# First chunk of the attention stage: shorter warming, decay factors broadcast in pieces, one large constant copied on the chip, loads and first products in another order

## Chip, cores and metric

The kernel runs on one core of one Trainium2 chip. The metric is device microseconds of one execution; the figure for a kernel is the median of its timed runs.

## What is computed

Attention with a decaying state over 768 tokens (2 batches, 8 heads of 64), then two layers of experts with routing. Only the first part is touched by the change.

```python
gamma = 1.0 - 2.0 ** (-5.0 - np.arange(H))            # one decay per head
for t in range(S):
    state = gamma * state + outer(k[:, :, t], v[:, :, t])
    y[:, :, t] = scale * einsum('bhd,bhde->bhe', q[:, :, t], state)
x = _moe_ref(x=y, ...)       # top-1 expert of 8, skip where x @ w_skip <= 0
out = _moe2_ref(x=x, ...)    # top-1 expert of 8 with a capacity per expert
```

## The kernel before

The attention works in 6 chunks of 128 tokens. For a chunk `c` and a batch `b`, `scores` (L622) multiplies keys and queries of the 8 heads: 8 products of 64 rows by 128 columns, in fp32, which the trace shows as 16 records, into two PSUM tiles `s` (4 heads each). VectorE multiplies each of the two with a decay mask (`p`, L631). `outs` (L672, from the second chunk on also L663) multiplies `p` with the values, ScalarE copies the result to `xt` (L679). `state` (L646) adds keys times values to the PSUM tile `u`, and ScalarE copies that to `sbd` (L653) for the next chunk. A generator (`sink`, of the routing) takes a finished chunk and puts its products between those of the next: `logits` (L389, copied by ScalarE to `lgs`, L393), sums (L399), transposes (L407).

The order on every engine is the order of the program text (`manual_schedule`); each engine takes its instructions in order and waits where a semaphore says so. Loads are issued by SP's queue (`nc.sync`) and by ScalarE's (`nc.scalar`); eight semaphores for loads are handed out in turn, and a load that gets one again waits in its queue for the load that had it before. A PSUM tile `s` takes one of four banks. Which one is fixed when the program is built.

What stands at the start of the program:

- ScalarE's queue issues two rows of 512 decay factors (`grow`, L107) and the columns with the triangle, the decays by position `GV` and by chunk `GS` of the constants `cs` (L108, 200 columns). SP's queue issues queries and keys of chunk 0 (L100, one load for each batch), values and keys with tokens first (L102).
- VectorE clears `zb`; TensorE then makes 7 products of `zb` with itself (`warm`, L548, 512 columns in bf16), whose results are not used.
- TensorE multiplies a column of ones with each of the two rows (`grow`), so that the decay factors stand on all 128 partitions (L571, two products of 512 columns with one row, fp32). VectorE makes the 8 masks from them (L573). A product of `zb` clears `u` (L577).
- `scores(0, 0)`; then `main(0, 0)`: `constants` (L143 to L147: the 512 columns `GQ` of query decays, 256 KB; the other 584 columns of constants; `wgt`; `cap_i`; one row of `table`), then queries and keys of chunk 1 (L77), then the further loads; `scale_k` (L598) and `decays` (L608) on GpSimd; `scores(0, 1)`, `outs(0, 0)`.
- `main(0, 1)`: `outs(0, 1)`, `state(0)`, `scores(1, 0)`.

Of the kernel before, what the change touches and what calls it, by code (L numbers as in the profile page):

```python
# [7 lines left out]
F32 = mybir.dt.float32  # L8
# [3 lines left out]
ACTF = mybir.ActivationFunctionType  # L12
# [29 lines left out]
def kernel(  # L42
# [12 lines left out]
    nc = tc.nc  # L55
# [18 lines left out]
    def load_qk(c, a_p):  # L74

        t = qk_tile(a_p)
        nc.sync.dma_start(out=t, in_=qkv[c, :, 0:2])  # L77
        return t
# [24 lines left out]
        return qk, kv  # L103

    grow = a_p.tile([128, 512], F32, name="grow", bufs=1)
    for i in (0, 64):
        nc.scalar.dma_start(out=grow[i:i + 1, :], in_=cst[i:i + 1, C_GQ:C_GQ + 512])  # L107
    nc.scalar.dma_start(out=cs[:, C_MASK:C_ID], in_=cst[:, C_MASK:C_ID])  # L108
    first = load_first()
    wgt = const.tile([128, KT, 32], F32, name="wgt")  # L110
    cap_i = const.tile([1, 2], I32, name="cap_i")
    zb = const.tile([128, 2 * RW], BF16, name="zb")
    nc.vector.memset(zb, 0.0)
    ones = const.tile([128, 128], BF16, name="ones")
    nc.vector.memset(ones, 1.0)
    a0 = const.tile([128, RW], F32, name="a0")

# [22 lines left out]
    ids_0 = const.tile([128, 2], I32, name="ids_0")  # L140

    def constants():
        nc.sync.dma_start(out=cs[:, C_GQ:C_MASK], in_=cst[:, C_GQ:C_MASK])  # L143
        nc.sync.dma_start(out=cs[:, C_ID:C_N], in_=cst[:, C_ID:C_N])
        nc.sync.dma_start(out=wgt, in_=wg)
        nc.sync.dma_start(out=cap_i, in_=capacity.bitcast(I32))
        nc.sync.dma_start(out=table[0:1, :], in_=zb[0:1, :].bitcast(F32))  # L147
# [397 lines left out]
    def warm(acc, n):  # L545

        for _ in range(n):
            nc.tensor.matmul(out=acc, lhsT=zb[:, 0:128], rhs=zb[:, 0:512], start=True, stop=True)  # L548


    def attention(a_p, ps, first, sink, pump, take_kv, give_kv, grow):
        units = [(c, b) for c in range(NCH) for b in range(B)]
        qk, kv, pt, xt = {}, {}, {}, {}
        sbd = [a_p.tile([128, B, 4, 128], F32, tag=f"sbd{i}", name="sbd", bufs=1) for i in range(2)]
# [3 lines left out]
        def psum(tag="m", bufs=2):  # L558
            return ps.tile([128, 512], F32, tag=tag, bufs=bufs, name=tag)
# [1 line left out]

        u = ps.tile([128, B, 4, D], F32, tag="u", bufs=1, name="u")
        if pump:
            warm(psum("s", 4), 7)

        mask = a_p.tile([128, 2, 4, 128], F32, name="mask", bufs=1)
        row1 = a_p.tile([128, 128], F32, name="row1", bufs=1)
        nc.gpsimd.memset(row1, 1.0)
        for j in range(2):
            g = psum("s", 4)  # L570
            nc.tensor.matmul(out=g, lhsT=row1[64 * j:64 * j + 1, :], rhs=grow[64 * j:64 * j + 1, :], start=True, stop=True)  # L571
            for r in range(4):
                nc.vector.scalar_tensor_tensor(  # L573
                    out=mask[:, j, r, :], in0=g[:, 128 * r:128 * r + 128], scalar=cs[:, C_GV + 2 * r + j:C_GV + 2 * r + j + 1],
                    in1=cs[:, C_MASK:C_MASK + 128], op0=ALU.mult, op1=ALU.mult,
                )
        nc.tensor.matmul(  # L577
            out=u.rearrange("p b r e -> p (b r e)"), lhsT=zb[:, 0:128], rhs=zb[:, 0:512], start=True, stop=True, skip_group_check=True
        )
        side, sunk = [], set()  # L580

        def step_side(c, b):
# [103 lines left out]
        def main(c, b):  # L686
            if b == 0:
                if c == 0:
                    if pump:
                        constants()  # L690
                        derived()
                    qk[1] = load_qk(1, a_p)
                    scale_k(0)
                    decays(1)
                if c + 1 < NCH:
                    kv[c + 1] = load_kv(c + 1, take_kv())
                if c + 2 < NCH:
                    qk[c + 2] = load_qk(c + 2, a_p)
                if pump and c:
                    kept[0] = c < NCH - 1  # L700
                    load_w()
                yield from scores(c, 1)
                if c and c + 1 < NCH:
                    decays(c + 1)
                if c == 0 and pump:
                    derived_late()
                if c:
                    yield from state(c)
                yield from outs(c, 0)
                return  # L710
            if c == 0:
                yield from outs(c, 1)
                yield from state(c)
            if c + 1 < NCH:
                yield from scores(c + 1, 0)
            if c:
                yield from outs(c, 1)
            give_kv(kv.pop(c))

        for _ in scores(0, 0):  # L720
# [5 lines left out]
            for _ in g:  # L726
                pass

    attention(a_p, psa, first, route_tokens(rowc, a_p), pump, take_kv, give_kv, grow)
    at.close()  # L730
    later[0] = 0

# [397 lines left out]
    def general(gctx):  # L1130
# [15 lines left out]
        with (  # L1146
            tc.tile_pool(name="ga", bufs=2) as ga_p,
            tc.tile_pool(name="gps", bufs=2, space=bass.MemoryType.PSUM) as gps,
        ):
            def take():  # L1150
                return ga_p.tile([128, 2, B, 512], F32, tag="kv", name="kv")

            grow = cs[:, C_GQ:C_GQ + 512]
            attention(ga_p, gps, (load_qk(0, ga_p), load_kv(0, take())), sink, None, take, lambda t: None, grow)
        ps = gctx.enter_context(tc.tile_pool(name="ps2", bufs=2, space=bass.MemoryType.PSUM))

        def psum(tag="t", bufs=2):
# [166 lines left out]
```

## Time and profile before

| | us |
|---|---|
| median of 3 timed runs | 398.36 |
| lowest and highest | 397.52, 399.19 |
| the profiled execution | 395.72 |
| its span, first to last instruction | 393.9 |

The profiled execution takes 1.8 us more than its span; the sums that follow are made against it. Times in the rows are microseconds from the start of the span. The lines that are read from its page and its trace stand in a section of their own below. In them PE is TensorE's products and PEld its loading of weights, DVE is VectorE, ACT ScalarE, POOL GpSimd, and SPq and ACTq are the queues of SP and ScalarE that issue loads.

### The profile page before, as it was taken

The page shows a single profiled execution, that of the slowest core. Times are in us where ns is not written, and L with a number is a line of the kernel's source. Part 1 is how long each engine was busy: PE and PEld are TensorE (multiplying, and loading weights), DVE is VectorE, ACT ScalarE, POOL GpSimd, SP SyncE. Part 2 cuts the span into 40 slices and gives each one's busy share as a digit, 9 for nine tenths or more (in the row PEclk, how much of TensorE's full clock was granted, in tenths as well). Part 3 has the DMA queues.
Part 4 walks back from the last instruction along what each step waited for, and adds up shares of the span by engine and source line. Part 5 has one row for each costly group of instructions (what it writes and reads, how often), then busy time and mean ns, then how long its engine had stood idle before and what let it go on. Part 6 is the DMA issues. An engine that isn't in the chain of part 4 may idle for free. (4 is left out here: it accounts for less than half of the span.)

```text
span 393.9 us, 6866 instructions
## 1 busy us (share of the span) xinstructions
PE 376.5 (96%) x2664; PEld 309.0 (78%) x2664; DVE 244.8 (62%) x437; ACT 210.5 (53%) x319; POOL 119.9 (30%) x184
## 2 busy tenths in 40 slices
PE   8999999899989999998999999999999999999992
PEld 4788887786667677676567998989989898898981
DVE  3657767498889869869535964654826476373200
ACT  1435655388778748747326753636636465462201
POOL 3678854262504402202143201304022040311102
PEclk9999999999999999999999999999999999999997
DMA  8999973899999998889844773965739377110101
GB/s 303 416 419 404 333 251 146 278 329 376 347 426 351 303 352 307 286 314 311 292 162 117 264 276 113 277 245 175 252 136 342 126 229 275 61 54 5 48 3 41
DMA packets 18175, 95.98 MB, mean 244 GB/s; under 512 B 2449, under 2 KB 2705, under 8 KB 8664
## 3 DMA queue, kind: packets, MB, share of 16 engines
q1 hardware_dynamic: 12196, 80.85, 56.5%
q0 software_dynamic: 3280, 9.76, 8.0%
q10 hardware_dynamic: 2660, 4.86, 3.3%
q8 instruction: 23, 0.38, 0.4%
q14 instruction: 16, 0.13, 0.1%
HBM read 87.03 MB, written 9.48 MB: 245 GB/s over the span
## 5 line engine op out<-in xcount | busy, mean ns | idle before, releaser
L251 DVE TENSOR_TENSOR lo<-big,hi 128x1024 fp32r<-128x1024 f32 (+1 forms) x126 | 147.5, 1185 | 60.9 <-ACT hi L248 60.0
L248 ACT ACTIVATE hi<-big 128x1024 fp32r<-128x1024 f32 (+1 forms) x126 | 124.6, 1013 | 3.8 <-DMA big<-in_w2a_dram 1.7
L784 PE MATMUL s<-xh,lo 128*128 128x256 f32 x224 | 63.4, 283 | 0.0
L783 PE MATMUL s<-xl,hi 128*128 128x256 f32 x224 | 63.4, 283 | 0.0
L782 PE MATMUL s<-xh,hi 128*128 128x256 f32 x224 | 63.4, 283 | 0.0
L905 POOL DMA_INDIRECT out_dram<-y,ixo x16 | 18.6, 1162 | 142.4 <-ACT y L900 139.4
L782 PE MATMUL o<-hi,hTh 128*128 128x512 f32 x112 | 44.9, 401 | 0.0
L783 PE MATMUL o<-lo,hTh 128*128 128x512 f32 x112 | 44.4, 396 | 0.0
L784 PE MATMUL o<-hi,hTl 128*128 128x512 f32 x112 | 44.4, 396 | 0.0
L782 PEld LDWEIGHTS s<-xh,hi 128*128 128x128 f32 x224 | 42.9, 191 | 0.3
L783 PEld LDWEIGHTS s<-xl,hi 128*128 128x128 f32 x224 | 42.9, 191 | 0.3
L784 PEld LDWEIGHTS s<-xh,lo 128*128 128x128 f32 x224 | 42.9, 192 | 0.0
L1084 ACT ACTIVATE hTh<-s 128x512 fp32r<-128x512 f32 x28 | 16.8, 598 | 41.0 <-PE s L784 41.0
L1085 DVE SCALAR_TENSOR_TENSOR hTl<-s,hTh 128x512 fp32r<-128x512 f32 x28 | 19.3, 691 | 30.5 <-ACT hTh L1084 30.3
L790 PE MATMUL s<-hi,xh 128*128 128x512 f32 x80 | 34.3, 429 | 1.6 <-DVE xl L377 0.9
L900 ACT ACTIVATE y<-o,rowc 128x512 f32<-128x512 f32 (+1 forms) x15 | 10.1, 674 | 47.6 <-issue 30.6
L790 PE MATMUL s<-lo,xh 128*128 128x512 f32 x80 | 31.5, 394 | 0.0
L879 POOL TENSOR_SCALAR rhsb<-m,cs 128x8 bf16<-128x8 bf16 x8 | 2.5, 306 | 81.1 <-DVE se L320 76.6
L790 PE MATMUL o<-hi,hTh 128*128 128x512 f32 x64 | 26.6, 415 | 0.0
L790 PE MATMUL o<-lo,hTh 128*128 128x512 f32 x64 | 25.3, 396 | 0.0
L784 PEld LDWEIGHTS o<-hi,hTl 128*128 128x128 f32 x112 | 21.1, 188 | 5.1
L790 PE MATMUL s<-hi,xl 128*128 128x512 f32 x80 | 25.1, 394 | 0.0
(162 smaller groups left out, 635.6 us busy)
## 6 DMA issues: line engine op xcount, KB each, us to landing
big<-in_w1a_dram SPq DMA_DIRECT2D x16, 1024.0 KB, 7.7
big<-in_w2a_dram SPq DMA_DIRECT2D x16, 1024.0 KB, 7.2
big<-in_w1b_dram SPq DMA_DIRECT2D x16, 1024.0 KB, 7.1
big<-in_w2b_dram SPq DMA_DIRECT2D x16, 1024.0 KB, 5.1
qk<-in_qkv_dram SPq DMA_DIRECT2D x5, 1024.0 KB, 10.2
big<-in_qkv_dram SPq DMA_DIRECT2D x5, 1024.0 KB, 12.0
table<-rowc ACTq DMA_DIRECT2D x5, 516.0 KB, 6.3
table<-row ACTq DMA_DIRECT2D x8, 258.0 KB, 7.2
```

The lines of the kernel that those rows point to most:

```text
L248: nc.scalar.activation(out=hi[:, k], in_=r3[:, k], func=ACTF.Copy)
L251: nc.vector.tensor_tensor(out=lo[:, k], in0=r3[:, k], in1=hi[:, k].bitcast(F32), op=ALU.subtract)
L782: nc.tensor.matmul(out=acc, lhsT=a[0], rhs=w[0], start=first, stop=False)
L783: nc.tensor.matmul(out=acc, lhsT=a[0], rhs=w[1], start=False, stop=False)
L784: nc.tensor.matmul(out=acc, lhsT=a[1], rhs=w[0], start=False, stop=last)
L790: nc.tensor.matmul(out=acc, lhsT=a, rhs=w, start=first and i == 0, stop=last and i == len(todo) - 1)
L879: nc.gpsimd.tensor_scalar(out=rhs[:, 0, :], in0=m, scalar1=p1, scalar2=None, op0=ALU.mult)
L900: nc.scalar.activation(out=y[:, 0:n], in_=acc[:, 0:n], func=ACTF.Copy, scale=xs[:, GCOL + 1:GCOL + 2])
L905: new = nc.gpsimd.indirect_dma_start(out=out[:, :], out_offset=bass.IndirectOffsetOnAxis(ap=ix, axis=0), in_=y, in_offset=None, bounds_che ...
L1084: nc.scalar.activation(out=hi[:, g:g + 2, :], in_=acc, func=ACTF.Relu)
L1085: nc.vector.scalar_tensor_tensor(out=lo[:, g:g + 2, :], in0=acc, scalar=0.0, in1=hi[:, g:g + 2, :].bitcast(F32), op0=ALU.max, op1=ALU.subtract
```

## The change

Five edits, all in the first chunk.

- `warm` makes 3 products, and the product that clears `u` follows directly.
- The rows `grow` come by one load of two rows, issued behind the constants that the masks need; that load holds 136 columns (triangle and the 8 columns of `GV` of chunk 0). The two broadcasts are made as four products of 256 columns, the first halves of both tiles first. The masks are made in turn for the one tile and the other. The column of ones (`row1`) is set by VectorE.
- The 512 columns `GQ` are no longer loaded: ScalarE copies them from the two broadcast tiles (two copies of 64 partitions by 512). The other constants come in one load of 648 columns, `GS` and the further `GV` with them.
- Queries and keys of chunk 1 are issued ahead of the constants, in two loads.
- In the first chunk `state(0)` stands behind `scores(1, 0)`.

```diff
+    nc.scalar.dma_start(out=cs[:, C_MASK:C_GV + 8], in_=cst[:, C_MASK:C_GV + 8])
+    nc.scalar.dma_start(out=grow[0:128:64, :], in_=cst[0:128:64, C_GQ:C_GQ + 512])
-    for i in (0, 64):
-        nc.scalar.dma_start(out=grow[i:i + 1, :], in_=cst[i:i + 1, C_GQ:C_GQ + 512])
-    nc.scalar.dma_start(out=cs[:, C_MASK:C_ID], in_=cst[:, C_MASK:C_ID])
...
     def constants():
-        nc.sync.dma_start(out=cs[:, C_GQ:C_MASK], in_=cst[:, C_GQ:C_MASK])
-        nc.sync.dma_start(out=cs[:, C_ID:C_N], in_=cst[:, C_ID:C_N])
+        nc.sync.dma_start(out=cs[:, C_GV + 8:C_N], in_=cst[:, C_GV + 8:C_N])
...
-            warm(psum("s", 4), 7)
-        ...
-        for j in range(2):
-            g = psum("s", 4)
-            nc.tensor.matmul(out=g, lhsT=row1[64 * j:64 * j + 1, :], rhs=grow[64 * j:64 * j + 1, :], start=True, stop=True)
-            for r in range(4):
-                nc.vector.scalar_tensor_tensor(...)      # mask[:, j, r] from g[:, 128 r:...]
+            warm(psum("s", 4), 3)
         nc.tensor.matmul(
             out=u.rearrange("p b r e -> p (b r e)"), lhsT=zb[:, 0:128], rhs=zb[:, 0:512], start=True, stop=True, skip_group_check=True
         )
+        g = [psum("s", 4) for j in range(2)]
+        for r in (0, 2):
+            for j in range(2):
+                nc.tensor.matmul(
+                    out=g[j][:, 128 * r:128 * r + 256], lhsT=row1[64 * j:64 * j + 1, :],
+                    rhs=grow[64 * j:64 * j + 1, 128 * r:128 * r + 256], start=True, stop=True,
+                )
+        for r in range(4):
+            for j in range(2):
+                nc.vector.scalar_tensor_tensor(...)      # mask[:, j, r] from g[j]
+        if pump:
+            for j in range(2):
+                pp = slice(64 * j, 64 * j + 64)
+                nc.scalar.activation(out=cs[pp, C_GQ:C_GQ + 512], in_=g[j][pp, :], func=ACTF.Copy)
...
                 if c == 0:
+                    qk[1] = qk_tile(a_p)
+                    for i in range(B):
+                        nc.sync.dma_start(out=qk[1][:, :, i], in_=qkv[1, :, 0:2, i])
                     if pump:
                         constants()
                         derived()
-                    qk[1] = load_qk(1, a_p)
...
             if c == 0:
                 yield from outs(c, 1)
-                yield from state(c)
             if c + 1 < NCH:
                 yield from scores(c + 1, 0)
             if c:
                 yield from outs(c, 1)
+            else:
+                yield from state(c)
```

On TensorE, from the broadcasts to the first products with values, with what each instruction waits for (DMAHW is a load, DVE is VectorE). L622 are the first and the second score of chunk 0, L672 the products with values. Before:

```order
L571 MATMUL s<-grow,row_137 128x512 [waits DMAHW0_49,Pool_49]
L571 MATMUL s<-grow,row_137 128x512 [waits DMAHW2_49]
L577 LDWEIGHTS zb
L577 MATMUL u<-zb 128x512
L622 MATMUL s<-qk 128x128 [waits DMAHW1_49]
L622 MATMUL s<-qk 128x128 [waits PE_49]
L622 MATMUL s<-qk 128x128 x6
L622 MATMUL s<-qk 128x128 [waits DMAHW3_49,DVE_49,PE_49]
L622 MATMUL s<-qk 128x128 [waits DVE_49,PE_49]
L622 MATMUL s<-qk 128x128 x6
L672 MATMUL m<-p,big_85 64x128 [waits DMAHW5_49,DVE_49]
L672 MATMUL m<-p,big_85 64x128 [waits DVE_49]
```

After, with L629 for the scores and L679 for the products with values:

```order
L565 MATMUL u<-zb 128x512
L573 MATMUL s<-grow,row_103 128x256 [waits DMAHW2_49,DVE_49]
L573 MATMUL s<-grow,row_103 128x256 x3
L629 MATMUL s<-qk 128x128 [waits DMAHW1_49]
L629 MATMUL s<-qk 128x128 [waits PE_49]
L629 MATMUL s<-qk 128x128 x6
L629 MATMUL s<-qk 128x128 [waits DMAHW3_49,DVE_49]
L629 MATMUL s<-qk 128x128 [waits DVE_49]
L629 MATMUL s<-qk 128x128 x6
L679 MATMUL m<-p,big_85 64x128 [waits DMAHW4_49]
L679 MATMUL m<-p,big_85 64x128 x7
```

The second score waits for VectorE in both, for another instruction of it: before, the program gives it the banks of the two broadcasts, and its wait is for the masks; after, it gives it the two banks of the first score, and its wait is for the two masked products of batch 0. The products with values of batch 0 waited for these masked products before and have no such wait left.

On ScalarE, at the start. Before:

```order
L107 DMA grow<-in_cst_dram 1x512 x2
L108 DMA cs<-in_cst_dram 128x200
L163 ACT_TABLE_LOAD
L163 ACTIVATE lc<-cs 128x256 [waits DMAHW0_49]
L679 ACTIVATE xt<-m 128x512 [waits PE_49] x2
```

After:

```order
L106 DMA cs<-in_cst_dram 128x136
L107 DMA grow<-in_cst_dram 2x512
L586 ACT_TABLE_LOAD [waits DVE_49]
L586 ACTIVATE cs<-s 64x512 [waits PE_49]
L586 ACTIVATE cs<-s 64x512 [waits DVE_49,PE_49]
L163 ACTIVATE lc<-cs 128x256 [waits DMAHW0_49]
L686 ACTIVATE xt<-m 128x512 [waits PE_49] x2
```

The two copies stand ahead of `lc`, and the load of ScalarE's table now stands behind a wait for VectorE's masks.

On SP's queue, the loads of chunk 1 and the constants. Before:

```order
L102 DMA big_85<-in_qkv_dram 128x1024 x2
L143 DMA cs<-in_cst_dram 128x512
L144 DMA cs<-in_cst_dram 128x584
L145 DMA wgt<-in_wg_dram 128x128
L146 DMA cap_i<-in_capacity_dram 1x2
L147 DMA table<-zb 1x516
L77 DMA qk<-in_qkv_dram 128x2048
```

After:

```order
L102 DMA big_85<-in_qkv_dram 128x1024 x2
L698 DMA qk<-in_qkv_dram 128x2x512 x2
L144 DMA cs<-in_cst_dram 128x648
L145 DMA wgt<-in_wg_dram 128x128
L146 DMA cap_i<-in_capacity_dram 1x2
L147 DMA table<-zb 1x516
L82 DMA big_86<-in_qkv_dram 128x2048
```

The 1 MB of chunk 1 stands ahead of the constants, and the load of 256 KB is gone.

## Rows read from the trace of the kernel before

**Rows 1.** Page: span; busy time, share of the span and instructions of each engine.

```profile
span 393.9 us, 6866 instructions
...
PE 376.5 (96%) x2664; PEld 309.0 (78%) x2664; DVE 244.8 (62%) x437; ACT 210.5 (53%) x319; POOL 119.9 (30%) x184
```

**Rows 2.** Stretches: length, busy time (instructions) of PE, PEld, DVE, ACT, POOL, PEclk, DMA, GB/s.

```profile
6.50:9.80 3.30, 3.30 (x27) 2.81 (x27) 2.75 (x9) 0.00 (x0) 0.89 (x1) 1.00 1.06 401
...
16.00:60.00 44.00, 43.65 (x599) 36.66 (x600) 31.14 (x86) 23.10 (x52) 33.82 (x42) 1.00 0.93 357
60.00:394.00 334.00, 318.55 (x1936) 263.36 (x1934) 207.53 (x334) 182.60 (x259) 79.58 (x120) 0.99 0.64 224
```

**Rows 3.** Waits of the whole run: who waited for whom, total, times, longest.

```profile
PEld t L860 <- DVE row L846: 6.2, 7, 1.5
...
PE t L860 <- DVE row L846: 4.0, 6, 1.1
```

**Rows 4.** TensorE in order of time: start, length, line, shape, count.

```profile
1.45 3.17 PE L548 MATMUL s<-zb 128*128 128x512 bf16 x7 [1.45 <-DVE zb L113]
4.55 2.08 PE L571 MATMUL s<-grow,row 1*128 1x512 f32 x4
6.56 0.61 PE L577 MATMUL u<-zb 128*128 128x512 bf16 x1
7.10 3.52 PE L622 MATMUL s<-qk 64*128 64x128 f32 x32
...
16.15 0.59 PE L399 MATMUL s<-zsum,lgs 128*128 128x18 f32 x4 [0.34 <-ACT lgs L393]
...
22.84 1.16 PE L622 MATMUL s<-qk 64*128 64x128 f32 x16
```

**Rows 5.** TensorE, order of time, window 7.09 to 8.9: the first score alone.

```profile
7.10 2.08 PE L622 MATMUL s<-qk 64*128 64x128 f32 x16
```

**Rows 6.** Score line L622, shortest, median, longest ns: window 7 to 9.7, then 13 to 20.

```profile
L622 PE MATMUL s<-qk x23: 417/418/579, 7.1 to 9.6; 64*128 64x128 f32 x23
```
```profile
L622 PE MATMUL s<-qk x32: 272/272/373, 13.9 to 18.3; 64*128 64x128 f32 x32
```

**Rows 7.** TensorE's weight loads in order of time: products with values, batches 0 and 1.

```profile
10.54 1.06 PEld L672 LDWEIGHTS m<-p,big 128*64 128x64 f32 x18
11.93 0.74 PEld L672 LDWEIGHTS m<-p,big 128*64 128x64 f32 x13 [0.32 <-DVE p L631]
```

**Rows 8.** VectorE in order of time: masks, masked products of chunk 0 and of chunk 1.

```profile
6.66 2.16 DVE L573 SCALAR_TENSOR_TENSOR mask<-s,cs 128x128 f32<-128x128 f32 x8 [5.12 <-PE s L571]
9.21 2.67 DVE L631 TENSOR_TENSOR p<-s,mask 128x512 f32<-128x512 f32 x4 [0.39 <-PE s L622]
...
15.84 1.29 DVE L631 TENSOR_TENSOR p<-s,mask 128x512 f32<-128x512 f32 x2 [3.40 <-PE s L622]
```

**Rows 9.** ScalarE in order of time, its queue's loads among it.

```profile
0.73 0.79 ACTq L107 DMA_DIRECT2D grow<-in_cst_dram  x2
...
1.94 1.28 ACT L163 ACT_TABLE_LOAD   x1 [1.94 <-issue]
10.24 0.42 ACT L163 ACTIVATE lc<-cs 128x256 bf16<-128x256 f32 x1 [7.02 <-DMA cs<-in_cst_dram]
11.68 0.60 ACT L679 ACTIVATE xt<-m 128x512 f32<-128x512 f32 x1 [1.03 <-PE m L672]
```

**Rows 10.** GpSimd in order of time: key scaling, decays of chunk 1.

```profile
8.91 2.04 POOL L598 TENSOR_TENSOR big<-big,cs 128x512 f32<-128x512 f32 x2 [5.82 <-DMA big<-in_qkv_dram]
10.91 1.04 POOL L608 TENSOR_TENSOR gqc<-cs 128x512 f32<-128x512 f32 x1
```

**Rows 11.** Loads by line: count, KB each, median us from issue to landing.

```profile
qk<-in_qkv_dram SPq DMA_DIRECT2D x2, 512.0 KB, 3.8
```

**Rows 12.** SP's queue in order of time: start and length of its first two issues.

```profile
0.73 0.95 SPq L100 DMA_DIRECT2D qk<-in_qkv_dram  x2
```

More of the change, by code (lines that the diff above doesn't have):

```diff
@@ L114 @@
     ones = const.tile([128, 128], BF16, name="ones")
+    row1 = a_p.tile([128, 128], F32, name="row1", bufs=1)
+    nc.vector.memset(row1, 1.0)
     nc.vector.memset(ones, 1.0)
@@ L548, in warm, with attention @@
             nc.tensor.matmul(out=acc, lhsT=zb[:, 0:128], rhs=zb[:, 0:512], start=True, stop=True)
-    def attention(a_p, ps, first, sink, pump, take_kv, give_kv, grow):
+    def attention(a_p, ps, first, sink, pump, take_kv, give_kv, grow, row1):
         units = [(c, b) for c in range(NCH) for b in range(B)]
@@ L563, in attention @@
         if pump:
-            warm(psum("s", 4), 7)
-        mask = a_p.tile([128, 2, 4, 128], F32, name="mask", bufs=1)
-        row1 = a_p.tile([128, 128], F32, name="row1", bufs=1)
-        nc.gpsimd.memset(row1, 1.0)
-        for j in range(2):
-            g = psum("s", 4)
-            nc.tensor.matmul(out=g, lhsT=row1[64 * j:64 * j + 1, :], rhs=grow[64 * j:64 * j + 1, :], start=True, stop=True)
-            for r in range(4):
[L573 to L576, printed above, removed]
+            warm(psum("s", 4), 3)
         nc.tensor.matmul(
@@ L579, in attention @@
         )
+        mask = a_p.tile([128, 2, 4, 128], F32, name="mask", bufs=1)
+        g = [psum("s", 4) for j in range(2)]
[7 more added lines that the diff above has]
+            for j in range(2):
+                nc.vector.scalar_tensor_tensor(
+                    out=mask[:, j, r, :], in0=g[j][:, 128 * r:128 * r + 128], scalar=cs[:, C_GV + 2 * r + j:C_GV + 2 * r + j + 1],
+                    in1=cs[:, C_MASK:C_MASK + 128], op0=ALU.mult, op1=ALU.mult,
+                )
+        if pump:
+            for j in range(2):
+                pp = slice(64 * j, 64 * j + 64)
+                nc.scalar.activation(out=cs[pp, C_GQ:C_GQ + 512], in_=g[j][pp, :], func=ACTF.Copy)
         side, sunk = [], set()
@@ L727, in attention @@
                 pass
-    attention(a_p, psa, first, route_tokens(rowc, a_p), pump, take_kv, give_kv, grow)
+    attention(a_p, psa, first, route_tokens(rowc, a_p), pump, take_kv, give_kv, grow, row1)
     at.close()
@@ L1151, in take @@
                 return ga_p.tile([128, 2, B, 512], F32, tag="kv", name="kv")
+            row1 = ga_p.tile([128, 128], F32, name="row1", bufs=1)
+            nc.vector.memset(row1, 1.0)
             grow = cs[:, C_GQ:C_GQ + 512]
-            attention(ga_p, gps, (load_qk(0, ga_p), load_kv(0, take())), sink, None, take, lambda t: None, grow)
+            attention(ga_p, gps, (load_qk(0, ga_p), load_kv(0, take())), sink, None, take, lambda t: None, grow, row1)
         ps = gctx.enter_context(tc.tile_pool(name="ps2", bufs=2, space=bass.MemoryType.PSUM))
```

## Prediction

> **What bounds the kernel now.** First the busy shares: TensorE is busy for 376.5 of 393.9 us, VectorE for 62% [rows 1]. Then the stretches: from 16 us on TensorE is busy in 43.65 of 44 us and in 318.55 of 334 us [rows 2]. Its largest waits are for routing rows that VectorE makes, 6.2 and 4.0 us in all on its two rows [rows 3], and these come out of TensorE's own earlier products. So nothing behind the first chunk takes up a delay: what the first 16 us gain or lose, the end gains or loses. Last I read the first 16 us in order of time. There the chain is: broadcasts from 4.55, masks from 6.66 to 8.82, masked products of the first score from 9.21, TensorE's products with values of batch 0 at 10.54 and of batch 1 at 11.93, the latter behind a wait for VectorE [rows 4, 7, 8]. The two scores run at half speed: a record takes 417 ns against 272 later, and a whole score 2.08 us against 1.16 [rows 4 to 6]. The seven warming products take about 0.43 us each (3.17 us for seven, the last one's end counted in) [rows 4], which is 512 columns at 1.2 GHz; the later scores run at 2.4. The column of granted clock says 1.00 there all the same [rows 2], so here I read the level from the lengths.
>
> **The change part by part.** Times are those of the profiled execution (395.72 us, span 393.9); I take the difference over to the median of 398.36.
>
> *Warming and the broadcasts.* Four warming products fewer are 1.7 us of TensorE work, but the broadcasts start at 4.55 and there is no row that shows whether they waited for the seventh product or for the second row of factors. That row was the second load of ScalarE's queue and is again the second load there [rows 9], so I keep 4.55 and let TensorE stand from about 3.2 on. Bounds: at best the broadcasts start at 3.2, 1.35 us earlier; at worst the factors land with the second half of the first queries, which is issued at about 1.2 [rows 12] and takes 3.8 us or more [rows 11]: landing at 5.0 to 5.9, 0.5 to 1.4 us later. Four products of 256 columns are as many columns as two of 512: no change. Halving them starts no mask earlier, since the first mask waits for its whole tile; the program counts the wait to the third of the four products. The masks therefore end at 8.82 as before (6.66 + 2.16). Clearing `u` earlier lets the first score start at 6.56 in place of 7.10 and end at 6.56 + 2.08 = 8.64, ahead of the masks. So the masked products of batch 0 start at 8.82, not 9.21, and two of them take 1.29 us [rows 8]: they end at 10.11. So far 0.39 us gained.
>
> *The new wait.* The second score now writes the banks of the first, and so waits for these masked products: its first products may start about 9.5, the rest at 10.11. Before, it followed the first score without a pause (32 records in 3.52 us) [rows 4]. Queued behind it on TensorE are the products with values, and VectorE's masked products of batch 1 wait for it. At the lower clock the score ends at 10.11 + 2.08 = 12.19, at the higher at 10.11 + 1.16 = 11.27. Add 1.29 for the masked products: 13.48 or 12.56, and 0.05 for the hand-over, as between 10.50 and 10.54 before. The products of batch 1 then start at 13.53 or 12.61 against 11.93: 1.60 or 0.68 us lost. The products of batch 0 fill the gap between: 1.06 us at the higher clock [rows 7], up to twice that at the lower, where they end some 0.3 us behind the masked products.
>
> *Which clock.* The trace shows one rise, at about 9.8 us within the second score, after products without a pause since 6.56, with 417 ns up to 9.6 [rows 4, 6]. In the changed kernel TensorE stands at about 3.2 to 4.5 and again from 8.4 to 10.1, so I take the rise to come behind the second score. The Trainium skill, TensorE: Matmul & The Clock Gate, Part 1, says that the low clock is the default, that sustained activity releases it, and that the point is not tied to the kernel's start; this trace agrees as far as one rise at 9.8 can. By that rule the pause costs the low clock for the second score (400.0 below), by the row alone, the same moment, it would not (398.7).
>
> *First states behind the next score.* TensorE stood 0.34 us before L399 for the `lgs` copy, which ScalarE made behind four `sbd` copies [rows 4]. With the states behind the logits, the copy is made while the states run: 0.34 us gained. The score of chunk 1 no longer comes in two halves around the logits; no other cost.
>
> *Queries ahead of the constants, 256 KB less.* The constants land at about 10.2 now (`lc` waited for them) [rows 9]. One MB ahead of them costs about 2.6 us at 401 GB/s [rows 2], the dropped 256 KB give back 0.6: about 12.2. `lc` then ends at 12.6 and the two `xt` copies queue behind it; the first now starts at 11.68 [rows 9], the logits need the second, which can't start before 14.4 here. Hidden; if the new wait did not exist, `lc` would be just in time. GpSimd waits for the same load with the decays of chunk 1: from 12.2, 1.04 us, then three short sums, done by about 14.2; the query scaling has the score of chunk 1 to wait for, about 15.6; the scaling of keys, 8.91 to 10.95, stays as it is [rows 10]. The earlier queries are used only because that score is moved forward. Less traffic gives nothing: TensorE waits for no load in the 16 to 60 us where the queues are full [rows 2].
>
> *The copies of decays.* ScalarE's table load, 1.28 us and out of the way at 1.94 before [rows 9], stands behind the last but one mask (8.6); two copies of at most 0.6 each follow: done near 11.1. Their readers are the decays (12.2) and the score of chunk 1 (14.4), which takes those two banks. Nothing; uncovered it would be up to 1.3 us.
>
> Sum: 1.60 - 0.34 = 1.26 us later, 0.3 more for the products of batch 0 at the low clock: 1.6. In the profiled execution 397.3, on the median 400.0. Its own bounds: 1.2 if the rise comes just behind the second score, 2.5 if the low clock also covers the products of batch 1 and part of the next score (a score there costs 0.92 more): 399.6 to 400.9.
>
> **The rivals.**
> - *The clock rises at the same moment.* Then 0.68 - 0.34 = 0.34 us lost: 398.7. For it: the first score still runs before 9.8; the trace can't say what the rise needs. Against: two pauses that were not there.
> - *The factors land early.* The broadcasts follow the fourth product at 3.2 and everything moves 1.35 us forward: 1.6 - 1.35, or with the early rise 0.34 - 1.35, gives 398.6 to 397.4, say 398.0. For it: the two loads are small; against: the first queries, 512 KB, are issued with them and take 3.8 us.
> - *Slower: the factors land late.* Issued behind a load of 128 pieces, they land with the second half of the first queries, at 5 to 6 us. From a landing past 4.9 on, each tenth goes straight into masks, masked products and second score; an estimate in the middle is 1.6 + 1.0, 401.0, up to 401.7. For it: the load engines are full from 6.5 us on (1.06) [rows 2]. Against: the place in ScalarE's queue is the same.
> - *The change does less than it says*, in that the masks start no earlier, is part of the forecast.
>
> **How the numbers follow.** Forecast 0.45 (400.0), same moment of the rise 0.22 (398.7), factors early 0.08 (398.0), factors late 0.25 (401.0). A measurement of this kernel tells about 0.5% from no change, 2.0 us: 396.4 to 400.35. Slower than that: nearly all of the late case, 0.24, and the upper third of the forecast's bounds, 0.14: 0.38. Faster: an early landing with an early rise and more than I see, 0.03. The rest, 0.59, is the same. The range goes from 398.2, half of the early case and a little of the same-moment case left out, to 401.7, the end of the late case.
>
> **What would show it.** In the trace after: the masks end at about 8.8 (they start with the third broadcast's end); the second score starts only behind the second masked product, with TensorE standing more than 1 us ahead of it; the length of its records (417 or 272 ns) tells the clock; no wait of L399 for `lgs`; `lc` at about 12.2 with nobody waiting for it; the table load behind the masks. It would be wrong if the second score follows the first without a pause, if the broadcasts start before 4 or behind 5, or if the distance at 16 us is not that at the end.

## The result, and the profile after

The changed kernel takes 399.98 us (median), the kernel before 397.49 beside it on the same chip: ratio 1.0059, with an interval of 1.0035 to 1.0082, so 1.4 to 3.3 us and most likely 2.3 us slower (the two medians lie 2.5 apart). The forecast was 1.6 us slower. The profiled execution took 397.37 us (span 395.6), 1.65 us more than the one of before (395.72), but it is the lowest of the kernel's 19 times, so its span is no second confirmation of the 1.6.

The page of after, its span and busy shares (compare [rows 1]), then the longest waits (compare [rows 3]). Line numbers have moved: L860, L846 are now L870, L856; L622, L672, L631 are L629, L679, L638; L571 is L573, L573 is L579.

```profile
span 395.6 us, 6872 instructions
PE 375.8 (95%) x2664; PEld 310.0 (78%) x2664; DVE 243.6 (62%) x438; ACT 211.9 (54%) x321; POOL 120.4 (30%) x183
```
```profile
PE t L870 <- DVE row L856: 3.2, 6, 1.0
PE s L573 <- DMA grow<-in_cst_dram: 2.8, 1, 2.8
...
PE s L629 <- DVE p L638: 0.8, 1, 0.8
```

Two of the three waits are new: for the factors, 2.8 us, and for VectorE's masked products, 0.8 us. The place is seen in TensorE's first 20 us in order of time (start, length, line, shape, count, idle time before it and who ended it), against [rows 4, 5, 7]:

```profile
6.17 2.08 PE L573 MATMUL s<-grow,row 1*128 1x256 f32 x8 [2.83 <-DMA grow<-in_cst_dram]
8.18 2.08 PE L629 MATMUL s<-qk 64*128 64x128 f32 x16
11.06 2.67 PE L629 MATMUL s<-qk 64*128 64x128 f32 x16 [0.80 <-DVE p L638]
13.66 2.44 PE L679 MATMUL m<-p,big 128*64 128x128 f32 x32
16.03 1.16 PE L629 MATMUL s<-qk 64*128 64x128 f32 x16
...
18.77 0.62 PE L399 MATMUL s<-zsum,lgs 128*128 128x18 f32 x4
...
19.97 0.66 PE L407 MATMUL s<-cs,xt 128*128 128x128 f32 x4
```

The broadcasts start at 6.17 and not at 4.55, behind the factors' load. The second score no longer follows the first but starts 0.80 us behind it. The router's logit sums (L399) wait no more for `lgs`. The router's transposes (L407) start at 19.97, against 17.31 before: 2.66 us later. These transposes are the mark by which the runs below are compared. VectorE and ScalarE beside it ([rows 8, 9]):

```profile
8.25 2.16 DVE L579 SCALAR_TENSOR_TENSOR mask<-s,cs 128x128 f32<-128x128 f32 x8 [6.58 <-PE s L573]
10.32 1.28 DVE L638 TENSOR_TENSOR p<-s,mask 128x512 f32<-128x512 f32 x2
13.36 1.29 DVE L638 TENSOR_TENSOR p<-s,mask 128x512 f32<-128x512 f32 x2 [1.76 <-PE s L629]
```
```profile
1.22 1.09 ACTq L107 DMA_DIRECT2D grow<-in_cst_dram  x1
10.23 1.28 ACT L586 ACT_TABLE_LOAD   x1 [10.23 <-DVE mask L579]
11.53 1.21 ACT L586 ACTIVATE cs<-s 64x512 f32<-64x512 f32 x2
12.76 0.42 ACT L163 ACTIVATE lc<-cs 128x256 bf16<-128x256 f32 x1
```

The four masked products stood in one row of 2.67 us before; now 1.76 us lie between the pairs, in which VectorE waits for the second score. ScalarE's two copies and its table load stand behind the masks. TensorE waits for none of them; GpSimd's decays of chunk 1 do, 1.62 us, but no product waits for these.

### The profile page after: what moved, and what is told of

Same layout as the page of the kernel before. It is cut to its first block, busy times and chain, and to the rows that moved or that the text cites. A ratio compares the mean times of both kernels' runs of the same rounds, so it can differ in the third digit from the quotient of the medians.

```text
span 395.6 us, 6872 instructions
## 1 busy us (share of the span) xinstructions
PE 375.8 (95%) x2664; PEld 310.0 (78%) x2664; DVE 243.6 (62%) x438; ACT 211.9 (54%) x321; POOL 120.4 (30%) x183
```

## The experiments

A profile is one execution; a time with its interval is from many. "Transposes" is the start of the router's transposes in the profile, 17.31 in the kernel before and 19.97 in the changed one.

### The bank wait: taken out, and put in alone

In the changed kernel the broadcasts take banks of the other tag:

```diff
-        g = [psum("s", 4) for j in range(2)]
+        g = [psum() for j in range(2)]
```

> The changed kernel with its two broadcast tiles in the two banks of the outputs, so that the second score gets banks of its own. Theory (the second score waits for the masked products only because of the banks): it follows the first without a pause, near 10.2 us in place of 11.06 to 11.65, the products with values of batch 1 start near 13.7 in place of 14.8, and the time falls by about 1 us (ratio to the kernel before 1.003 to 1.004). Rival (the wait is hidden behind the late masks): the products with values of batch 1 start within 0.3 us of before and the time stays at 1.006.

TensorE in order of time in this run:

```profile
7.96 3.79 PE L629 MATMUL s<-qk 64*128 64x128 f32 x32
11.95 2.58 PE L679 MATMUL m<-p,big 128*64 128x128 f32 x32 [0.21 <-ACT cs L586]
...
18.39 0.66 PE L407 MATMUL s<-cs,xt 128*128 128x128 f32 x4
```

The two scores are one row of 32 products again, though the factors are as late as in the changed kernel (the first score at 7.96, there at 8.18). The transposes come 1.58 us earlier, and the time is 397.26 us, ratio 0.9996 (0.9969 to 1.0023). The time falls by more than expected (1.003 to 1.004): at the transposes 1.08 us of the loss are left, which the time does not show. The other half of the test is the kernel before with this wait and nothing else:

```diff
-            sa = [psum("s", 4), psum("s", 4)]
+            sa = held.pop() if (c, b) == (0, 1) else [psum("s", 4), psum("s", 4)]
+            if not c and not b:
+                held.append(sa)
```

> The kernel before with the new wait alone: the second score of the first chunk is written into the two banks of the first one, everything else as it was. Theory (the forecast's step on the wait): the first score from 7.10, masks to 8.82, masked products of batch 0 9.21 to 10.5; the second score begins 9.85 with one bank and goes on at 10.5 with the other, at the low clock to 12.6, masked products of batch 1 to 13.9, products with values of batch 1 at 13.95 against 11.93: 2.0 us later there and at the transposes (19.3), and 1.5 to 2.0 us in the whole time, ratio 1.004 to 1.005. Rival A (the wait costs no clock, the rise stays near 10 us): second score 10.5 to 11.7, products of batch 1 at 13.05, 1.1 us later, ratio 1.003. Rival B (a delay in the first 16 us is taken up later): transposes 2 us late, time the same within 0.2%.

```profile
9.95 2.67 PE L624 MATMUL s<-qk 64*128 64x128 f32 x16 [0.78 <-DVE p L633]
12.55 3.48 PE L674 MATMUL m<-p,big 128*64 128x128 f32 x32
...
20.34 0.66 PE L407 MATMUL s<-cs,xt 128*128 128x128 f32 x4
```

The score starts and lasts as forecast. The products with values take 3.48 us (2.44 in the changed kernel, 3.68 in a run below, just behind a stretch with a granted clock of 0.50), so they lie mostly at the low level too, and the transposes are 3.03 us late and not 2.0. Since the rise of the clock moves from execution to execution (last section), this one profile does not show how much of the further 1.0 us is the wait's. The time is 1.0034 (1.0003 to 1.0065), 0.1 to 2.6 us: slower, as forecast, but the interval holds rival A's 1.003 too; it is the 2.67 us of the second score, at the low level, that speak against that rival. Both halves say that the wait is real. By the middle of the intervals, taking it out gives back all that the change lost (1.0059 to 0.9996), and put in alone it costs a little over half of it.

### The late factors: place, form, and both costs out

The two single rows ahead of the constants again, as before the change:

```diff
+    for i in (0, 64):
+        nc.scalar.dma_start(out=grow[i:i + 1, :], in_=cst[i:i + 1, C_GQ:C_GQ + 512])
     nc.scalar.dma_start(out=cs[:, C_MASK:C_GV + 8], in_=cst[:, C_MASK:C_GV + 8])
-    nc.scalar.dma_start(out=grow[0:128:64, :], in_=cst[0:128:64, C_GQ:C_GQ + 512])
```

> The changed kernel with its two rows of decay factors loaded as before: two loads, first in ScalarE's queue, the constants behind them. Theory (the factors came late because they stand behind the constants' load): the broadcasts start near 4.55 us in place of 6.17, the masks end near 8.8 in place of 10.41, the second score starts at 10.1 in place of 11.06 to 11.65, and the time falls by 1.0 to 1.6 us against the changed kernel (ratio to the kernel before 1.002 to 1.004). Rival (the place in the queue is not the cause): the broadcasts stay at 6 us and the time at 1.006.

```profile
6.60 2.08 PE L630 MATMUL s<-qk 64*128 64x128 f32 x16
9.45 2.67 PE L630 MATMUL s<-qk 64*128 64x128 f32 x16 [0.78 <-DVE p L639]
12.05 3.29 PE L680 MATMUL m<-p,big 128*64 128x128 f32 x32
...
19.21 0.66 PE L408 MATMUL s<-cs,xt 128*128 128x128 f32 x4
```
```profile
1.54 0.36 ACTq L108 DMA_DIRECT2D cs<-in_cst_dram  x1
```
```profile
6.44 2.17 DVE L580 SCALAR_TENSOR_TENSOR mask<-s,cs 128x128 f32<-128x128 f32 x8 [4.77 <-DMA cs<-in_cst_dram]
```

(The last two rows are of ScalarE's queue and of VectorE.) Broadcasts, masks and first score move forward by 1.6 us and more, the masks now behind their constants; the bank wait stays (0.78 us). The transposes come at 19.21, only 0.76 us earlier than in the changed kernel: the products with values now lie mostly ahead of the clock's rise and take 3.29 us in place of 2.44. Ratio 1.0048 (1.0015 to 1.0081), which can't be told from the changed kernel's, nor from the expected 1.002 to 1.004: here the trace decides and not the time. Next, the one load of both rows kept, but put first:

```diff
+    nc.scalar.dma_start(out=grow[0:128:64, :], in_=cst[0:128:64, C_GQ:C_GQ + 512])
     nc.scalar.dma_start(out=cs[:, C_MASK:C_GV + 8], in_=cst[:, C_MASK:C_GV + 8])
-    nc.scalar.dma_start(out=grow[0:128:64, :], in_=cst[0:128:64, C_GQ:C_GQ + 512])
```

> The changed kernel with its one load of both rows of factors put ahead of the load of masks and decays on ScalarE's queue: place and form of that load told apart. Theory (place: it came late because it stood behind 128 pieces): it lands by 4.5, as the two single rows did (4.44 before, 4.56 with the rows first), all four broadcasts lie between 3.2 and 6.4, masks 6.3 to 8.5 behind the other load, the bank wait as with the rows first (second score 9.3 to 9.5). Rival (form: one load that takes both rows from 64 partitions apart is slow by itself): it lands at 5.5 or later, as in the changed kernel (6.03, 5.81 and 5.86 in its three profiles), the masks start at 7.6 or later and the second score at 10.4 or later.

TensorE, ScalarE's queue and VectorE in this run:

```profile
4.47 2.08 PE L573 MATMUL s<-grow,row 1*128 1x256 f32 x8 [1.14 <-DMA grow<-in_cst_dram]
```
```profile
0.73 1.11 ACTq L106 DMA_DIRECT2D grow<-in_cst_dram  x1
1.89 0.36 ACTq L107 DMA_DIRECT2D cs<-in_cst_dram  x1
```
```profile
8.20 2.16 DVE L579 SCALAR_TENSOR_TENSOR mask<-s,cs 128x128 f32<-128x128 f32 x8 [6.53 <-DMA cs<-in_cst_dram]
```

The factors are there at 4.47: the place made them late, as the theory has it. The trace's records of the single packets on ScalarE's queue show the same: in the changed kernel the 128 pieces of the constants start from 2.56 to 4.20 and the two rows of factors only at 5.30 and 5.41; here both rows start at 3.8. The form seems to cost too: the issue of this load takes 1.11 us, against 0.79 for both single loads [rows 9], and the load behind it is then issued at 1.89 (1.54 with the single rows). The masks wait for that load until 8.20, against 6.44 with the rows first. By the packets, 0.5 of these 1.76 us are a later start (5.18, and 4.68 with the rows first); for the rest its 128 pieces take longer, to 7.57 in place of 5.90, and why is open in this one execution. Nothing is won: the transposes come 0.97 us later than in the changed kernel; the one execution took 399.14 us. Last, rows first and own banks together (the two diffs above):

> The changed kernel with both suspected costs taken out at once: the factors come as two loads of one row each ahead of the constants, and the broadcasts take the two banks of the other tag, so that the second score needs not wait for the masked products of the first. Theory (the loss is the late factors plus the bank wait, and the two add up): with the rows at 4.5 and the constants at 6.3, as with the rows alone, masks 6.4 to 8.6, first score 6.6, second score directly behind it at 8.6 to 8.7, and from there the distances of the run with own banks (9.24 us from the first score to the router's logit sums): logit sums at 15.8, transposes at 17.0, 0.3 us ahead of before (17.31) and 1.4 ahead of the run with own banks alone (18.39). Time 0.3 us under before, ratio 0.997 to 1.000. Rival A (the start of the first chunk gives nothing to the end, as the run with own banks, whose transposes were 1.1 us late and whose time was that of before, suggests): the time is that of the run with own banks, 1.000, though the transposes come 1.4 us earlier. Rival B (the queries of chunk 1 or the constants, which land at 11.7 to 13, come too late for the earlier work): TensorE stands before the score of chunk 1 and the transposes stay at 17.6 or later.

```profile
6.36 3.79 PE L630 MATMUL s<-qk 64*128 64x128 f32 x32
10.15 2.46 PE L680 MATMUL m<-p,big 128*64 128x128 f32 x32
...
16.71 0.66 PE L408 MATMUL s<-cs,xt 128*128 128x128 f32 x4
```

Time 395.81 us, ratio 0.9963 (0.9939 to 0.9986): faster than the kernel before. This version beats both. With the two costs out, the rest of the change is worth 0.60 us at the transposes in this profile and 0.6 to 2.4 us in the time. Rival A has little left: over own banks alone the transposes gained 1.68 us and the ratio 0.0033, or 1.3 us, though the two intervals still overlap.

### The warming products and the clock

Three warming products in the kernel before, in place of seven; ten in the changed kernel, in place of three; six with rows first and own banks:

```diff
-            warm(psum("s", 4), 7)
+            warm(psum("s", 4), 3)
...
-            warm(psum("s", 4), 3)
+            warm(psum("s", 4), 10)
...
-            warm(psum("s", 4), 3)
+            warm(psum("s", 4), 6)
```

> The kernel before with 3 warming products in place of 7, nothing else. Theory (four products fewer cost clock now and then, but move no work): the broadcasts start at 4.55 as before, TensorE stands for 1.7 us ahead of them, and the time is 0 to 1 us above before (ratio 1.000 to 1.003). Rival (the seven products set the time of the rise): the rise comes behind the second score and the ratio is 1.004 or more.

> The changed kernel with 10 warming products in place of 3, so that TensorE works until the factors land. Theory (the pause from 3.2 to 6.2 us costs clock): the broadcasts still start at 6.2, but the records of the first or the second score shorten from 417 to 272 ns earlier than in the changed kernel, and the time falls by 1 to 2 us (ratio 1.001 to 1.004). Rival (warming products do not matter as long as the next pause follows): the second score has 417 ns records as in the changed kernel and the time stays at 1.006.

> The same with six warming products in place of three, so that TensorE works from 1.4 to 4.4 without a pause, into the landing of the second row of factors (4.5). Theory (the pause of the warming costs nothing by itself, since the masks are what the first score's products wait for): masks 6.4 to 8.6 and transposes as with three, within 0.4 us, and the same time within 0.2%. Rival (the pause costs the clock): the records turn from 417 to 272 ns ahead of the second score, near 8 to 10 us as before the change, and the second score, the products with values and what follows take up to 1.5 us less: transposes at 15.5 to 16.2, ratio 0.994 to 0.997.

Three in the kernel before: 397.54 us, ratio 0.9990 (0.9964 to 1.0016). Both broadcasts, the wait of the second for its row counted in, end at 6.6 as before (2.84 + 3.75; 4.55 + 2.08 in [rows 4]), and the transposes come at 17.61. So the missing four products cost nothing that can be measured in the time, as forecast; the 0.30 us at the transposes are a later rise of the clock in this profile (the two scores take 3.90 us in place of 3.52). Ten in the changed kernel, TensorE in order of time, then a stretch (columns as in [rows 2]; the granted clock is the third number from the end):

```profile
7.40 1.16 PE L629 MATMUL s<-qk 64*128 64x128 f32 x16
10.32 2.67 PE L629 MATMUL s<-qk 64*128 64x128 f32 x16 [1.75 <-DVE p L638]
12.91 3.68 PE L679 MATMUL m<-p,big 128*64 128x128 f32 x32
```
```profile
11.00:13.00 2.00, 2.00 (x17) 1.78 (x18) 0.39 (x1) 1.04 (x3) 0.54 (x1) 0.50 1.11 431
```

The clock is high for the first score (1.16 us against 2.08), then TensorE stands 1.75 us at the bank wait, and the granted clock is 0.50: the second score takes 2.67 us again. Ratio 1.0078 (1.0046 to 1.0110). More warming does not help while the wait is there. Six with own banks show the same with another wait:

```profile
4.48 1.13 PE L574 MATMUL m<-grow,row 1*128 1x256 f32 x8
5.54 2.06 PE L630 MATMUL s<-qk 64*128 64x128 f32 x32
10.19 2.78 PE L680 MATMUL m<-p,big 128*64 128x128 f32 x32 [2.59 <-ACT cs L587]
```
```profile
8.34 2.47 DVE L639 TENSOR_TENSOR p<-s,mask 128x512 f32<-128x512 f32 x4
```

Both scores run at the high level and are done by 7.6. Then the products with values, whose banks are those of the broadcasts, wait 2.59 us, at the end for ScalarE's copies, which stand behind the masks. Most of it is not the copies' own: the products also need the two masked products of batch 0, and these are done at 9.63 (8.34 + 1.29), 0.56 us before the copies let go. The transposes come at 17.63, 0.9 us later than with three; ratio 0.9966 (0.9937 to 0.9996), the same as with three. The rival's early rise came, and its gain went into that wait and the fall of the clock behind it.

### The order of the first states, alone

```diff
             if c == 0:
                 yield from outs(c, 1)
-                yield from state(c)
             if c + 1 < NCH:
                 yield from scores(c + 1, 0)
             if c:
                 yield from outs(c, 1)
+            else:
+                yield from state(c)
```

> The kernel before with one part of the change alone: the first states stand behind the score of chunk 1. Theory (as far as the forecast's 0.34 us go): the logit sums wait no longer for the copy of the logits, 0.34 us gained there; but the queries of chunk 1 land at 13.16 in the kernel before, and the score of chunk 1 would now be ready for them at 12.75, so TensorE stands some 0.4 us ahead of it: the transposes at 17.3 to 17.4, the time unchanged, ratio 1.000. Rival (the queries' first half is there early enough): the transposes at 16.95 and 0.3 us gained, ratio 0.999; the time can't tell these two apart, the trace can, by what stands ahead of the score of chunk 1.

397.13 us, ratio 0.9983 (0.9955 to 1.0010): no difference that can be measured, as expected. The wait for `lgs` is gone, but neither theory can be read from the transposes (17.80), because the clock rose later in this execution, in instructions that the edit doesn't touch. The score records of this run and of the kernel before, in the same stretch (9 to 11.1; shortest, median, longest ns):

```profile
L622 PE MATMUL s<-qk x20: 417/417/537, 8.6 to 10.7; 64*128 64x128 f32 x20
```
```profile
L622 PE MATMUL s<-qk x18: 271/417/542, 8.8 to 10.3; 64*128 64x128 f32 x18
```

The first row is of this run: no record is short. The second is of the kernel before, where the clock rises within the same score.

### Does a delay of the first chunk reach the end?

VectorE makes the first masks twice, then four times:

```diff
-            for r in range(4):
+            for r in list(range(4)) * 2:
                 nc.vector.scalar_tensor_tensor(
```

> The kernel before with VectorE's eight masks made twice over, a known delay: masks 6.66 to 10.98, masked products of batch 0 from 11.0 in place of 9.21, 1.8 us later; the two scores lie ahead of that as before. TensorE then stands from 10.0 to 12.3, so the products with values may run at the lower clock: transposes 1.8 to 3.3 us later. Theory (as the prediction has it: nothing behind the first chunk takes up a delay): the time grows by what the transposes are late, ratio 1.005 to 1.008. Rival (the wait for the second routing row, at 112 us, takes up to its 1.1 us of it, since it hangs on weights that come from memory at their own pace): the distance from the transposes to the first transposed row behind that wait shrinks by up to 1.1, ratio 1.002 to 1.005.

> The same with the masks made four times: masks 6.66 to 15.3, masked products of batch 0 from 15.35, 6.1 us later, transposes 6.1 to 7.6 us later. Theory (nothing takes up a delay): the time grows by all of it, ratio 1.015 to 1.019. Rival (the wait at 112 us gives back its 1.1 us and no more): the time grows by 5.0 to 6.5, ratio 1.0125 to 1.016, and the wait for the second routing row is gone. A third way (the stretch to 112 us is paced by the transfers throughout): most of the 6 us are given back, ratio under 1.01.

The transposes come at 20.95 and 24.75, 3.64 and 7.44 us later than before. The first is past the expected 1.8 to 3.3, the second within 6.1 to 7.6, but both by a way that was not expected: I had taken the second score to lie ahead of the repeated masks, but it takes the banks of the broadcasts, which the masks read, and waits (masks made twice):

```profile
11.07 2.04 PE L622 MATMUL s<-qk 64*128 64x128 f32 x14 [1.25 <-DVE mask L573]
```

The times are 1.0062 (1.0031 to 1.0093) and 1.0205 (1.0161 to 1.0249), that is 1.2 to 3.7 and 6.4 to 9.9 us. With the masks made twice the interval holds the theory and its rival. With four times, a delay of 7.44 us arrives in full within the interval, and the rival's 6.3 (1.1 given back) lies just outside it; that the transfers behind pace the kernel falls. The wait that might give back 1.1 us is still there with four masks, 1.2 us long:

```profile
PE t L860 <- DVE row L846: 1.2, 1, 1.2
```

Last, an attempt to gain at that end: rows first, own banks, six warming products, the masks' constants between the halves of the first queries, copies written over the factors' tile, the other constants ahead of the queries of chunk 1, and one more copy behind the attention. Its core:

```diff
+            if not b:
+                nc.sync.dma_start(out=cs[:, C_MASK:C_GV + 8], in_=cst[:, C_MASK:C_GV + 8])
...
-        for r in range(4):
-            for j in range(2):
+        for j in range(2):
+            for r in range(4):
                 nc.vector.scalar_tensor_tensor(
...
-                nc.scalar.activation(out=cs[pp, C_GQ:C_GQ + 512], in_=g[j][pp, :], func=ACTF.Copy)
+                nc.scalar.activation(out=grow[pp, :], in_=g[j][pp, :], func=ACTF.Copy)
```

> Rows first and own banks, and four steps further: six warming products; the load of masks and the first decays between the two halves of the first queries on SP's queue; broadcasts and masks of one group of heads ahead of the other's, with ScalarE's copies written over the factors' own tile, so that they wait for no mask; the other constants and the router's weights ahead of the queries of chunk 1. Theory (what the first chunk gains, the end gains): broadcasts 4.5 to 5.6, masks 5.2 to 7.4, first score from 5.6 at 272 ns a record, second score from 6.7, masked products of batch 0 7.4 to 8.7, products with values of batch 1 at 10.0, score of chunk 1 at 11.1, transposes 15.0 to 15.5 against 16.71 with rows and banks alone: 1.2 to 1.7 us less than that run, ratio 0.992 to 0.994. Rival (behind the first chunk the weights' transfers decide, as the wait at 112 us suggests, which was 0.28 us long in the changed kernel and 1.11 before): the transposes come as early, but the wait for the second routing row grows by most of it, and the ratio stays at 0.996.

```profile
4.54 2.16 PE L576 MATMUL m<-grow,row 1*128 1x256 f32 x8
```

396.32 us, ratio 0.9987 (0.9964 to 1.0011); transposes 16.76. The theory, with 15.0 to 15.5, missed by 1.3 to 1.8 us at the transposes, and neither it nor its rival was put to the test: the clock stayed low. The same six products as above were followed by broadcasts of 2.16 us here and of 1.13 us there.

## Why the prediction was right in its outcome, and where it was not

The bank wait that it made its forecast of is the one that the runs show; one term was wrong, and it lay in a rival. Two of its own signs of being wrong came: the broadcasts start behind 5, at 6.17, and the distance early on, 2.66 us at the transposes, is not that at the end, 1.65. So what came is the forecast's wait and the rival's late factors together.

- *Warming fewer, at no cost:* right (0.9990 with that part alone).
- *Broadcasts kept at 4.55:* wrong. They start at 6.17, 0.3 us past the worst bound of 5.9. This is the rival of the late factors, with a chance of 0.25. The prediction spoke against it with "the place in ScalarE's queue is the same". The place was the second in both, but before it stood behind a load of one row, and now behind one of 128 pieces; with the factors' load ahead of that one they come at 4.47. The Trainium skill, DMA: Bandwidth & Descriptors, section Issuing engines are not separate DMA queues, says that transfers issued by different engines run on the same 16 DMA engines and interleave; our trace agrees so far as packets of SP's queue (from 1.81 us) and of ScalarE's (from 2.56) run at the same time. What held the two rows until 5.30, though, is the load ahead of them on their own queue.
- *Masks end unchanged at 8.82, masked products 0.39 earlier:* the first follows from the broadcasts, and they end at 10.41 (8.25 + 2.16), not 8.82. That the first score is done ahead of them held: the masked products follow at 10.32 without a pause ([rows 8] had 0.39).
- *The new wait:* right, and nearly in size. From the first masked product of batch 0 to the last of batch 1 the forecast has 13.48 - 8.82 = 4.66 us; measured are 13.36 + 1.29 - 10.32 = 4.33. The 0.33 are an overlap that was overlooked: the masked products start at 13.36 on the first bank, while the score writes the other to 13.73 (11.06 + 2.67). The sign "standing more than 1 us" missed: TensorE stands 0.80 us, and the score starts when the first masked product has freed one bank, not behind the second one, which ends at 11.60 (10.32 + 1.28).
- *The clock rises behind the second score:* right in this profile, where the rival of the same moment is out. The records of the two scores are of 417 ns, those from 16 us on of 272. The reason given, the two pauses, isn't shown: with the order of the states alone, where TensorE has neither pause, the records of both scores were long as well. Nor do [rows 4] show products without a pause only since 6.56; they show them since 1.45.

```profile
L629 PE MATMUL s<-qk x32: 417/417/580, 8.2 to 13.3; 64*128 64x128 f32 x32
```
```profile
L629 PE MATMUL s<-qk x24: 272/272/373, 16.0 to 19.8; 64*128 64x128 f32 x24
```

- *0.34 us gained at the logit sums, 0.3 more for batch 0's products at the low clock:* the first is seen, L399 has no wait left. The second can't be seen by itself, since both batches' products are one row without a pause; these 32 products take 2.44 us, against 3.68 in the run with ten warming products, where the clock had fallen, so the rise lies near their start.
- *Constants at 12.2, table load behind the masks, copies done near 11.1:* the table load at 10.23, the copies done at 12.74 and `lc` at 12.76, each later with the masks, each waited for by nobody on the path. When the constants land can't be seen there, since `lc` stands behind the copies; with rows first and own banks it waits for them until 12.28, near the forecast (with rows first alone until 13.09):

```profile
12.28 0.42 ACT L164 ACTIVATE lc<-cs 128x256 bf16<-128x256 f32 x1 [1.57 <-DMA cs<-in_cst_dram]
```

- *Sum:* 1.6 forecast at the transposes; 2.66 measured there. The late factors add 1.5 (the first masked product at 10.32 and not at 8.82), the overlap gives back 0.33, and 0.1 is unexplained. That the late factors delay the chain by 1.5 does not make them worth 1.5: taken out alone they gave back 0.76, since the clock then rose later against the work. In the time it is 2.3 us (1.4 to 3.3), below the 2.6 that the late-factors rival gave, and its bounds hold both, so the time can't tell the forecast from that rival; the start of the broadcasts does. The single figure of 400.0 beside a median of 399.98 is luck in part: it owes its closeness to the kernel before, too, which took 397.49 beside it and not the 398.36 that the sum was added to.
- *"Nothing behind the first chunk takes up a delay":* right within what can be told for 7.44 us. It isn't strict: the wait for the second routing row, near 112 us, differs from execution to execution. In the changed kernel it was 0.3 us long, in the kernel before 1.1 (the longest in [rows 3]), with own banks 1.8; the rows of the changed kernel and of that with own banks, stretch 104 to 121:

```profile
PE t L870 <- DVE row L856: 0.3, 1, 0.3
```
```profile
PE t L870 <- DVE row L856: 1.8, 1, 1.8
```

The row comes out of VectorE, but not only out of TensorE's own products, as the prediction had it. VectorE makes it behind the splitting of weights, and ScalarE, ahead of that, waits for the weights' transfer. These lines of the kernel before show the chain (ScalarE, then VectorE):

```profile
108.71 2.01 ACT L248 ACTIVATE hi<-big 128x1024 fp32r<-128x1024 f32 x2 [0.72 <-DMA big<-in_w1a_dram]
```
```profile
109.80 1.22 DVE L251 TENSOR_TENSOR lo<-big,hi 128x1024 fp32r<-128x1024 f32 x1 [0.25 <-ACT hi L248]
110.94 0.74 DVE L846 SCALAR_TENSOR_TENSOR row<-o,rowc 128x512 f32<-128x512 f32 x1
```

This is most of why the profiled executions differ by 1.65 us at the end and 2.66 at the transposes: behind this wait they are 1.72 apart (111.74 and 113.46). What sets this wait in one execution is open: it was absent with the bank wait alone (3.03 us late at the transposes) and 1.2 us long with four masks (7.44 late).

## What to carry to other kernels

Where a buffer is read longer than before, look up which banks the next users get: here two copies that kept the broadcasts' banks busy sent the second score to the first one's (built without these copies, the program gives it the broadcasts' banks, as before), and other banks for the broadcasts took the change's loss away within what can be told. Before a load is called small, look at what stands ahead of it in its queue and how long its own issue takes. And take two edits out together as well as one by one: each alone gave 0.8 and 1.6 us at the transposes, both 3.3, and the clock rose at another place in each.

## What the hardware showed beyond that

- The moment of the clock's rise isn't set by the instructions alone. The kernel before and the one with the other order of the states issue the same to TensorE up to about 12.7 us; in one profile the records shorten within the second score, in the other none does. Six warming products were followed by four broadcasts of 1.13 us in one kernel and of 2.16 us in another. The Trainium skill, TensorE: Matmul & The Clock Gate, Part 1, says that the point of the rise isn't tied to the kernel's start; these four profiles agree, in that the same opening was followed by a rise at another time. A sum made from one profile carries that moment with it.
- After a stop of 1.75 us at the high level the granted clock was 0.50 and a score took 2.67 us again; after one of 2.59 us it was 0.54 from 11 to 13 us. Ahead of the first rise the column says 1.00 though the records have the length of the low level, so there the length has to be read.
- One load of two rows took 1.09 and 1.11 us to issue on ScalarE's queue, two loads of one row 0.79 us together.
